# Moving the last tile's query projection ahead of the products with wo, and stacking the few-column products of each wp block

## The chip, the core and the metric

The kernel runs on one core of a Trainium2 chip. A core has a TensorE (matrix products, from SBUF into PSUM), a VectorE, a ScalarE and a GpSimd (elementwise work), and a SyncE whose queue issues most DMAs. In the profile these are PE (with its weight loads as PEld), DVE, ACT, POOL and SP. Each engine takes its instructions strictly in the order of the program and meets the others through semaphores. The metric is the device time of the whole kernel in microseconds; less is better.

## The reference

Two branches over the same 2048 tokens of width 576 are mixed by a gate. Branch A is a linear attention with 32 heads of 18 columns; branch B is a layer norm and an MLP with 4608 hidden columns.

```python
def _A_ref(x, wqkv, wo):
    q, k, v = ...                       # (x @ wqkv), 32 heads of 18 columns
    phi = lambda t: jnp.where(t > 0, t + 1, jnp.exp(t)) + 1e-6
    pq, pk = phi(q), phi(k)
    kv = jnp.einsum("bhsd,bhse->bhde", pk, v)
    z = jnp.einsum("bhsd->bhd", pk)
    num = jnp.einsum("bhqd,bhde->bhqe", pq, kv)
    den = jnp.einsum("bhqd,bhd->bhq", pq, z)[..., None] + 1e-6
    return (num / den).transpose(...).reshape(B, S, D) @ wo
...
g = _sigmoid((x * gate_w).sum(-1, keepdims=True))
return g * _A_ref(...) + (1 - g) * _B_ref(...)   # _B_ref: layernorm, w1, gelu, w2
```

## The kernel before

**Stages.** The 2048 tokens are 16 tiles of 128 rows. The first stage (to about 184 us) goes over the tiles: it projects keys and queries, applies phi, and sums two things over all tokens: the keys (for z) and the products of x with the keys. From these sums, `kv = wv^T (x^T phi(k))` needs no values of single tokens. Then comes the short middle stage, which the change concerns (about 184 to 206 us): it makes the block-diagonal kv of each head, multiplies it with wo into one matrix wp of 576 x 576, and so folds the value product and the output projection into one. The attention loop (lines 900 to 912, 16 turns) then multiplies each tile's normalized queries with wp. After it the MLP runs as a Strassen-like scheme with seven products, in an order that a planner writes out; the change does not touch that, and the planner's costs are constants.

**Splitting.** Most large products are kept near float32 accuracy: each factor is the sum of a rounded high part and a low part, and three products (high by high, high by low, low by high, `TERMS`) are summed in PSUM. A high part is a ScalarE copy, a low part a VectorE subtraction.

**Groups and blocks.** The 576 columns of kv are cut into groups of `GW = 126` = 7 heads of 18, so that no head straddles a group: four groups of 126, and a fifth that is laid over the last 126 columns. wp is cut into five blocks of 128 rows (the last has 64, kept twice for its high and low parts). Block t takes its rows from group t and, since 128 > 126, a few from group t+1: 2, 4, 6 and 8 rows for t = 0 to 3. `PIECES` (line 573) lists these nine pairs. `mask_kv` (653) multiplies kv, read from PSUM, with a block-diagonal mask into `kvs`; `kv_low` (663) makes the low parts; `project_values(t)` (764) does, for each half of 288 output columns, three products for each of the block's pieces, so 12 matmuls a block and 6 for the last, each with a weight load. ScalarE and VectorE then take block t out of PSUM as the high and low parts of wp.

**The order in the middle stage** (lines 666 to 810). TensorE: the queries of tile `late[1]`, kv (733 to 737: 25 products in float32, each two records), `project_values(0..4)`, the transposes of tile 0, the queries of tile `late[2]` (lines 804, 805; the last of three tiles whose queries were left over), the transposes of tile 1, then the loop. `normalize(i)` (693) makes the denominator of tile i (reduce, add, reciprocal: part 0) and multiplies it into the queries (part 1, a scalar_tensor_tensor on VectorE); `tail_q(i)` (705) copies the last 64 columns twice on ScalarE; `transpose_q(i)` (776) transposes the queries on TensorE and splits them into `qt` (high on ScalarE, low and tail on VectorE); `queries_out(i)` (343) is phi: for each half two passes on ScalarE and one on VectorE. `weigh(i)` (687) on GpSimd multiplies queries with z for the denominator; `qz` has three buffers, so weigh(4) waits until the reduce of normalize(1) has read its buffer, and weigh(5) until that of normalize(2) has.

**PSUM.** There are eight banks. project_values takes pairs of banks in turn, (6, 7) and (4, 5), and a pair is free again when VectorE has taken block t out; transposes use (0, 1) and (2, 3); attend uses (6, 7) and (4, 5).

**SBUF reuse and the queues.** High and low parts of wo lie where the key weights were; high parts of kv lie in the first of the four places for x; the low parts in a place of a finished store. On the SP queue come, in order: wo (at job 40), the stores of y, `load_w1(0)` (762), then `load_y` (811) over the same place, which waits for the products with wo. GpSimd has `sum_keys` of the last tiles, then `weigh(0)`.

Of the kernel before, what the change touches and what calls it, by code (L numbers as in the profile page):

```python
# [31 lines left out]
ORDER = [sup * TPS + a * TPB + j for sup in range(NSUP) for j in range(TPB) for a in range(2)]  # L32
PLACE = [ORDER.index(i) for i in range(NT)]
# [5 lines left out]
LATE = 3  # L39
X_RING = 4  # L40
# [54 lines left out]
def raw(ap):  # L95
    return ap.bitcast(F32)
# [35 lines left out]
def tile_gated_mix(ctx: ExitStack, tc: tile.TileContext, x, xm, xe, wm, we, wvm, wve, wo, um, ue, w2, b1, b2, gw, out):  # L132
    nc = tc.nc
    pe, act, dve, pool = (InOrder(tc, e) for e in (nc.tensor, nc.scalar, nc.vector, nc.gpsimd))
    sp = InOrder(tc, nc.sync)
# [5 lines left out]
    ps = ctx.enter_context(tc.tile_pool(name="ps", bufs=1, space=PSUM)).tile([P, 8, 512], F32, name="ps")  # L141
    t_pairs, ff_banks, ff_pairs = cycle((0, 2)), cycle(range(4)), cycle((6, 4))

    def two_of(ring):
        n = next(ring)
        return ps[:, n:n + 2]
# [36 lines left out]
    mask = spare[:GW, 26 * P:26 * P + GW]  # L183
# [18 lines left out]
    QUERY, KEY = range(2)  # L202
    TERMS = ((0, 0), (0, 1), (1, 0))
    W, at_ = {}, 0
    for part in (KEY, QUERY):
        for half in range(2):
            n = HALF + 2 * (part == KEY and half)
# [3 lines left out]
    y_place = ym[:, at_ + X_RING * 9 * P:][:, :2 * 5 * P]  # L211
    x_places = [ym[:, at_ + n * 9 * P:at_ + (n + 1) * 9 * P].rearrange("p (a n) -> p a n", n=P) for n in range(X_RING)]
# [3 lines left out]
    wv = a1.enter_context(tc.tile_pool(name="wvp", bufs=1)).tile([P, 5, D], F32, name="wv")  # L216
# [73 lines left out]
    def project(i, part, half, order=BY_ROWS, n=None, between={}):  # L290
        w = W[part, half]
        p = banks[i, part, half] = ps[:, next(halves_in) if n is None else n]
        for m, (a, b) in enumerate(order):
            pe.matmul(p[:, :w.shape[2]], xs[i][:, a, :], w[:, b], start=(m == 0), stop=(m == len(order) - 1))
            if m in between:
                between[m]()
# [46 lines left out]
    def queries_out(i):  # L343
        for half in range(2):
            phi(acc[i], i, QUERY, half)
# [223 lines left out]
    wop_ = wop.enter_context(tc.tile_pool(name="wop", bufs=1, side="right"))  # L569
    wot = wop_.tile([GW, G, D], F32, name="wot")  # L570


    PIECES = [(t, j) for t in range(5) for j in (t, t + 1) if j < G]
    kvs = wop_.tile([GW, len(PIECES), P], F32, name="kvs")
    pool.memset(kvs, 0.0)
    ysc = ExitStack()
    ysp = ysc.enter_context(tc.tile_pool(name="ysp", bufs=1, side="right"))
    y_stages = [ysp.tile([P, 2, 5, P], F32R, name=f"ys{n}") for n in range(3)]
# [5 lines left out]
    def at(n, f, *args):  # L584
        jobs[n].append(lambda: f(*args))

    def load_wo():
        sp.dma_start(wot[:, 0:4], wo[0:4 * GW].rearrange("(t p) n -> p t n", p=GW))
        sp.dma_start(wot[:, 4], wo[D - GW:D])

    def load_wv():
        sp.dma_start(wv[:, 0:4], wvm.rearrange("p (t n) -> p t n", t=4))
        load_twice(wv[:, 4], wve)

    at(3 * 5, sp.dma_start, b1s, b1)
    at(9, load_wv)
    at(40, load_wo)
    for b, n in enumerate((9, 13, 22, 28)):
# [20 lines left out]
    for n in range(FIRST, NT):  # L619
        i, before = ORDER[n], ORDER[n - 1]  # L620
# [22 lines left out]

    late, end = ORDER[NT - LATE:], ORDER[-1]
    wo_parts = [ym[:GW, a * G * D:(a + 1) * G * D].rearrange("p (j n) -> p j n", j=G) for a in range(2)]
    kv_parts = [x_places[PLACE[late[0]] % X_RING - 1][:GW], y_place[:GW, :len(PIECES) * P].rearrange("p (t n) -> p t n", n=P)]

    def split_wo(j0, j1):
        hi, lo = (part[:, j0:j1] for part in wo_parts)
        act.activation(hi, wot[:, j0:j1], AF.Copy)  # L650
        dve.tensor_sub(lo, wot[:, j0:j1], raw(hi))

    def mask_kv(n0, n1):
        for n in range(n0, n1):
            t, j = PIECES[n]
            c0 = min(j * GW, D - GW)
            lo, hi = max(j * GW, t * P), min((j + 1) * GW, (t + 1) * P, D)
            own = slice(lo - c0, hi - c0)
            for at_ in (lo - t * P, lo - t * P + 64)[:1 + (t == 4)]:
                dve.tensor_tensor(out=kvs[:, n, at_:at_ + hi - lo], in0=kv[j][:, own], in1=mask[:, own], op=OP.mult)  # L660
        act.activation(kv_parts[0][:, n0:n1], kvs[:, n0:n1], AF.Copy)

    def kv_low(n0, n1):
        dve.tensor_sub(kv_parts[1][:, n0:n1], kvs[:, n0:n1], raw(kv_parts[0][:, n0:n1]))

    split_wo(0, 2)
    split_wo(2, 4)
    projected(late[0], QUERY)
    queries_out(late[0])
    split_wo(4, 5)  # L670
    moments_of(end)
    for part in range(2):
        add_products(end, part)
# [31 lines left out]
    def tail_q(i):
        tails[i] = small.tile([P, P], F32, name="tail")
        act.activation(halves(tails[i]), acc[i][:, None, 4 * P:D].to_broadcast([P, 2, 64]), AF.Copy)


    xk = spare[:, :5 * D].rearrange("p (t n) -> p t n", n=D)  # L710
# [19 lines left out]
    dve.tensor_scalar(den0, den0, EPS_PHI, EPS_PHI, op0=OP.mult, op1=OP.add)  # L730
    project(late[1], QUERY, 0, n=4)
    project(late[1], QUERY, 1, n=0)
    kv = [ps[:GW, 1 + j // 3, j % 3 * GW:(j % 3 + 1) * GW] for j in range(G)]
    for j in range(G):
        c0 = min(j * GW, D - GW)
        for t in range(5):
            pe.matmul(kv[j], wv[:, t, c0:c0 + GW], xk[:, t, c0:c0 + GW], start=t == 0, stop=t == 4)
    queries_out(late[1])
    for i in range(1, 3):
        weigh(i)  # L740
    normalize(0, (0,))
    mask_kv(0, 5)
    normalize(0, (1,))
    tail_q(0)
    kv_low(0, 5)
    mask_kv(5, 9)
    kv_low(5, 9)
    w_pairs = cycle((6, 4))

    def wr(k):  # L750
        at_ = fresh[:, :21 * P] if k > 1 else spare[:, :21 * P]
# [12 lines left out]
    def project_values(t):  # L764

        pw = two_of(w_pairs)
        own = [(n, j) for n, (to, j) in enumerate(PIECES) if to == t]
        for half in range(2):
            parts = [(kv_parts[a][:, n], wo_parts[b][:, j]) for a, b in TERMS for n, j in own]
            for m, (a, b) in enumerate(parts):  # L770
                pe.matmul(pw[:, half, :HALF], a, b[:, half_cols(half)], start=m == 0, stop=m == len(parts) - 1)
        p = pw[:, :, :HALF]
        act.activation(halves(wp[:, t]), p, AF.Copy)
        dve.tensor_tensor(out=halves(wp[:, 5 + t]), in0=p, in1=halves(raw(wp[:, t])), op=OP.subtract)

    def transpose_q(i):

        both = two_of(t_pairs)
        p, pe_ = both[:, 0].rearrange("p (g n) -> p g n", n=P), both[:, 1, :P]
        for t in range(4):  # L780
            pe.transpose(p[:, t, :], acc[i][:, t * P:(t + 1) * P], ident)
        pe.transpose(pe_, tails[i], ident)
        if i == LAST_SHARE:
            turn_moments(len(MOMENTS) - 1, both[:, 1, P:2 * P])
        q = qt[i] = qtp.tile([P, 9, P], F32R, name="qt")
        act.activation(q[:, 0:4], p, AF.Copy)
        if i == LAST_SHARE:
            store_moments(len(MOMENTS) - 1, both[:, 1, P:2 * P])
        act.activation(q[:, 4], pe_, AF.Copy)
        dve.tensor_sub(q[:, 5:9], p, raw(q[:, 0:4]))  # L790
        dve.scalar_tensor_tensor(q[:, 4], raw(q[:, 4]), low_half[:, 0:1], pe_, op0=OP.mult, op1=OP.add)

    project_values(0)
    normalize(1, (0,))
    project_values(1)
    project_values(2)
    project_values(3)
    normalize(1, (1,))
    project_values(4)
    tail_q(1)  # L800
    normalize(2, (0,))
    transpose_q(0)
    normalize(2, (1,))
    for half in range(2):
        project(late[2], QUERY, half, n=4 + half)
    transpose_q(1)
    tail_q(2)
    queries_out(late[2])
    a1.close()
    for m in [FACTORS[n][1] for n in UP_ORDER]:  # L810
        load_y(0, m)
# [874 lines left out]
```

## Time and profile before

| what | us |
|---|---|
| median of three runs (lowest, highest) | 1088.93 (1088.69, 1089.76) |
| the profiled execution's own time | 1087.51 |
| its span from first to last instruction | 1085.8 |
| PE busy (matmuls) | 1080.8 (100%) |
| PEld busy (weight loads) | 994.5 (92%) |
| DVE busy | 933.9 (86%) |
| ACT busy | 692.7 (64%) |
| POOL busy | 242.4 (22%) |

Times in the timeline count from the start of the span. A row of the timeline gives start, length, engine, operation, tiles, shape, count, and in brackets the idle time of the engine before it and who ended it. A row of the groups gives count, busy time, mean length of one in ns, and the idle time before. Nearly all lines are L125, a helper that records every operation, so rows are told apart by their tiles: `ps<-accs,wv` is kv, `ps<-y 126x288` the products with wo, `ps<-y 128x288` a query projection, `ps<-wp,qt` attend, `den<-qz` the reduce of normalize, `accs<-accs,den` its last step, `kvs<-ps,accs` the mask.

### The profile page before, as it was taken

To read this page: it belongs to the slowest core of one execution; us is meant where nothing else is said; L and a number is where in the kernel's file an instruction comes from. 1 tells how busy PE (TensorE), PEld (TensorE's weight loads), DVE (VectorE), ACT (ScalarE), POOL (GpSimd) and SP (SyncE) were. 2 spreads that over 40 slices of the span, in tenths; PEclk is the share of its full clock that TensorE was granted. 3 is DMA by queue.
4 is the path that set the end of the run, shared out by engine and by line. 5 is a ranking of instruction groups with operands and counts; after the bars stand their busy time and mean duration, and the time that the engine had idled before them with its cause. 6 is when DMAs were issued, how large, how long until landed. Compare 5 with 4: busy or idle time off the path is not lost.

```text
span 1085.8 us, 18609 instructions
## 1 busy us (share of the span) xinstructions
PE 1080.8 (100%) x6700; PEld 994.5 (92%) x6700; DVE 933.9 (86%) x1547; ACT 692.7 (64%) x1234; POOL 242.4 (22%) x226
## 2 busy tenths in 40 slices
PE   9999999999999999999999999999999999999998
PEld 9999999999898999998899989998999989999898
DVE  5568787895799999899999998988878888888898
ACT  7677766444668777778887785555545455455642
POOL 2111112431123231322323321121231132112100
PEclk9999999999999999999999999999999999999999
DMA  6356662735744746664656559764544445344432
GB/s 188 126 97 183 177 215 105 311 149 193 246 157 174 248 163 225 202 211 165 205 192 220 180 190 385 244 226 119 158 121 125 119 135 150 119 120 119 142 94 88
DMA packets 116062, 189.65 MB, mean 175 GB/s; under 512 B 8956, under 2 KB 79244, under 8 KB 111874
## 3 DMA queue, kind: packets, MB, share of 16 engines
q1 hardware_dynamic: 115074, 187.72, 53.6%
q8 instruction: 53, 0.87, 0.3%
q10 hardware_dynamic: 704, 0.74, 0.2%
q14 instruction: 39, 0.32, 0.1%
q0 software_dynamic: 192, 0.01, 0.1%
HBM read 121.63 MB, written 66.80 MB: 174 GB/s over the span
## 4 chain that ended last, share of the span: by engine, by line
PE 99%; DVE 0%; ACT 0%; issue 0%
PE ps L125 99%; DVE wp L125 0%; ACT wp L125 0%; DVE ystage L125 0%; DVE ones L125 0%
## 5 line engine op out<-in xcount | busy, mean ns | idle before, releaser
L125 PEld LDWEIGHTS ps<-region,h 128*128 128x128 f32 x3060 | 434.3, 188 | 25.2 <-issue 0.8
L125 PE MATMUL ps<-region,h 128*128 128x288 f32 x3060 | 450.7, 295 | 0.0
L125 DVE TENSOR_TENSOR accs<-ps,accs 128x576 f32<-128x576 f32 x337 | 249.5, 752 | 44.3 <-PE ps L125 37.5
L125 PE MATMUL ps<-y,wa 128*128 128x512 f32 x1008 | 254.9, 392 | 0.0
L125 PEld LDWEIGHTS ps<-y,wa 128*128 128x128 f32 x1008 | 181.9, 188 | 31.8
L125 PE MATMUL ps<-y,wb 128*128 128x512 f32 x756 | 198.6, 393 | 0.0
L125 DVE TENSOR_TENSOR h<-u,h 128x512 fp32r<-128x512 f32 x243 | 170.4, 721 | 7.3 <-ACT u L125 6.8
L125 POOL TENSOR_TENSOR fresh<-fresh 128x288 f32<-128x288 f32 (+1 forms) x99 | 87.5, 886 | 325.4 <-DVE h L125 99.0
L125 PEld LDWEIGHTS ps<-y,wb 128*128 128x128 f32 x756 | 133.8, 188 | 20.7
L125 POOL TENSOR_TENSOR u<-u 128x512 f32<-128x512 f32 x67 | 92.9, 1387 | 245.5 <-ACT u L125 57.9
L125 PE MATMUL ps<-y 128*128 128x288 f32 (+2 forms) x950 | 133.2, 297 | 0.2 <-DVE wp L125 0.2
L125 PEld LDWEIGHTS ps<-y 128*128 128x128 f32 (+1 forms) x950 | 129.7, 188 | 1.8 <-DVE wp L125 0.9
L125 ACT ACTIVATE ps<-ps 128x512 f32<-128x512 f32 (+1 forms) x129 | 79.9, 622 | 72.2 <-PE ps L125 45.0
L125 ACT ACTIVATE region<-fresh 128x576 fp32r<-128x576 f32 (+1 forms) x134 | 82.3, 624 | 62.5 <-PE ps L125 61.5
L125 ACT ACTIVATE u<-ps 128x512 f32<-128x512 f32 x73 | 43.4, 595 | 77.9 <-PE ps L125 76.7
L125 ACT ACTIVATE h<-u 128x512 fp32r<-128x512 f32 x132 | 77.7, 622 | 20.0 <-POOL u L125 10.6
L125 DVE TENSOR_TENSOR region<-fresh,region 128x576 fp32r<-128x576 f32 (+1 forms) x134 | 87.7, 684 | 0.0
L125 DVE TENSOR_TENSOR u<-ps,u 128x512 f32<-128x512 f32 x74 | 50.3, 681 | 15.1 <-PE ps L125 12.8
L125 PE MATMUL ps<-wp,qt 128*128 128x288 f32 x448 | 63.0, 297 | 0.0
L125 ACT ACTIVATE h<-u,b1s 128x512 fp32r<-128x512 f32 x73 | 52.5, 720 | 13.3 <-DVE u L125 12.9
L125 PEld LDWEIGHTS ps<-wp,qt 128*128 128x128 f32 x448 | 59.8, 188 | 0.0
L125 PE MATMUL ps<-ks,xs 128*128 128x448 f32 (+4 forms) x256 | 53.4, 354 | 0.0
(140 smaller groups left out, 1042.2 us busy)
## 6 DMA issues: line engine op xcount, KB each, us to landing
w1d<-wa SPq DMA_DIRECT2D x17, 1280.0 KB
wa<-w1d SPq DMA_DIRECT2D x68, 320.0 KB
fresh<-in_w SPq DMA_DIRECT2D x70, 288.0 KB
y<-yd SPq DMA_DIRECT2D x14, 1280.0 KB
w1d<-wb SPq DMA_DIRECT2D x17, 960.0 KB
wb<-w1d SPq DMA_DIRECT2D x51, 320.0 KB
fresh<-in_um SPq DMA_DIRECT2D x64, 128.0 KB
yd<-ys SPq DMA_DIRECT2D x12, 640.0 KB
```

Source lines behind the costliest of these rows:

```text
L125: self.last = self.tc.keep_in_program_order(op(*args, **kwargs))
```

## The change

1. The fifth group no longer overlaps the fourth: `SIZES` is 126, 126, 126, 126, 72. The kv product of the fifth group has 72 columns, and wo and kv are cut to match.
2. The three products with group t+1 become one. Its first 18 rows (one head) suffice. `rest_kv` and `rest_wo` hold three bands of 18 rows, at partitions 0, 32 and 64: kv high with wo high, kv low with wo high, kv high with wo low. One product over 96 rows sums all three. A block has 8 matmuls rather than 12; the last stays at 6.
3. `rest_wo` is first filled by GpSimd copies, twice (jobs 44 and 47, and again after `split_wo(4, 5)`), so that the rows between bands are defined; six DMAs on the SP queue (`gather_rest`) then bring the bands from the split wo. The rows of kv between bands are zeros.
4. `mask_kv` goes block by block and has one VectorE copy more for blocks 1 to 4; the few columns get ScalarE copies (two each call of `kv_high`) and a VectorE subtraction of their own.
5. The queries of `late[2]` go right behind kv on TensorE, to banks 0 and 3. Their phi, normalize(1) in one piece and tail_q(1) come ahead of the products with wo; normalize(2) in one piece comes behind them and ahead of the transposes of tiles 0 and 1, which now follow one another.
6. The products with wo take a third pair of banks in turn, (1, 2).

```diff
-    PIECES = [(t, j) for t in range(5) for j in (t, t + 1) if j < G]
-    kvs = wop_.tile([GW, len(PIECES), P], F32, name="kvs")
+    SIZES = [min(GW, D - j * GW) for j in range(G)]
+    kvs = wop_.tile([GW, G, P], F32, name="kvs")
     pool.memset(kvs, 0.0)
+    rest = wop_.tile([DH, G - 1, 8], F32, name="rest")
+    pool.memset(rest, 0.0)
+    rest_wo = wop_.tile([96, G - 2, D], F32R, name="rest_wo")
...
+    kv_place = x_places[PLACE[ORDER[NT - LATE]] % X_RING - 1]
+    rest_kv = kv_place[:96, G:]
+    rest_wo_last = y_place[:96, G * P:G * P + D]
+    at(44, pool.tensor_copy, rest_wo, wot[:96, :G - 2])
+    at(47, pool.tensor_copy, rest_wo_last, wot[:96, G - 2])
+    at(47, pool.tensor_copy, rest_kv, kvs[:96, :G - 1])
...
+    def gather_rest():
+        for at_, part in ((0, 0), (32, 0), (64, 1)):
+            sp.dma_start(raw(rest_wo[at_:at_ + DH]), raw(wo_parts[part][:DH, 1:G - 1]))
+            sp.dma_start(raw(rest_wo_last[at_:at_ + DH]), raw(wo_parts[part][:DH, G - 1]))
+
+    def mask_kv(t):
+        lo, hi = t * P - t * GW, min((t + 1) * P - t * GW, SIZES[t])
+        for at_ in (0, 64)[:1 + (t == 4)]:
+            dve.tensor_tensor(out=kvs[:SIZES[t], t, at_:at_ + hi - lo], in0=kv[t][:, lo:hi], in1=mask[:SIZES[t], lo:hi], op=OP.mult)
+        if t:
+            n = 2 * t
+            dve.tensor_copy(rest[:, t - 1, 8 - n:], kv[t][:DH, :n])
+
+    def kv_high(t0, t1):
+        n = SIZES[t1 - 1]
+        act.activation(kv_parts[0][:n, t0:t1], kvs[:n, t0:t1], AF.Copy)
+        r0, r1 = max(t0 - 1, 0), t1 - 1
+        for at_ in (0, 64):
+            act.activation(rest_kv[at_:at_ + DH, r0:r1, P - 8:], rest[:, r0:r1], AF.Copy)
...
     split_wo(4, 5)
+    pool.tensor_copy(rest_wo, wot[:96, :G - 2])
+    pool.tensor_copy(rest_wo_last, wot[:96, G - 2])
+    gather_rest()
+    pool.tensor_copy(rest_kv, kvs[:96, :G - 1])
...
+    for half in range(2):
+        project(late[2], QUERY, half, n=3 * half)
     normalize(0, (0,))
-    mask_kv(0, 5)
+    for t in range(3):
+        mask_kv(t)
     normalize(0, (1,))
+    mask_kv(3)
+    kv_high(0, 4)
     tail_q(0)
-    kv_low(0, 5)
-    mask_kv(5, 9)
-    kv_low(5, 9)
-    w_pairs = cycle((6, 4))
+    mask_kv(4)
+    kv_low(0, 4)
+    kv_high(4, 5)
+    kv_low(4, 5)
+    w_pairs = cycle((6, 4, 1))
...
-            parts = [(kv_parts[a][:, n], wo_parts[b][:, j]) for a, b in TERMS for n, j in own]
+            parts = [(kv_parts[a][:n, t], wo_parts[b][:n, t]) for a, b in TERMS]
+            if t < 4:
+                parts.append((rest_kv[:, t], rest_wo[:, t] if t < 3 else rest_wo_last))
...
-    project_values(0)
-    normalize(1, (0,))
-    project_values(1)
-    project_values(2)
-    project_values(3)
-    normalize(1, (1,))
-    project_values(4)
+    normalize(1)
     tail_q(1)
-    normalize(2, (0,))
-    transpose_q(0)
-    normalize(2, (1,))
-    for half in range(2):
-        project(late[2], QUERY, half, n=4 + half)
-    transpose_q(1)
+    queries_out(late[2])
+    for t in range(5):
+        project_values(t)
+    normalize(2)
+    for i in range(2):
+        transpose_q(i)
     tail_q(2)
-    queries_out(late[2])
```

More of the change, by code (lines that the diff above doesn't have):

```diff
@@ L588, in load_wo @@
         sp.dma_start(wot[:, 0:4], wo[0:4 * GW].rearrange("(t p) n -> p t n", p=GW))
-        sp.dma_start(wot[:, 4], wo[D - GW:D])
+        sp.dma_start(wot[:SIZES[4], 4], wo[4 * GW:D])
     def load_wv():
@@ L645, in tile_gated_mix @@
     wo_parts = [ym[:GW, a * G * D:(a + 1) * G * D].rearrange("p (j n) -> p j n", j=G) for a in range(2)]
-    kv_parts = [x_places[PLACE[late[0]] % X_RING - 1][:GW], y_place[:GW, :len(PIECES) * P].rearrange("p (t n) -> p t n", n=P)]
+    kv_parts = [kv_place[:GW, :G], y_place[:GW, :G * P].rearrange("p (t n) -> p t n", n=P)]
     def split_wo(j0, j1):
-        hi, lo = (part[:, j0:j1] for part in wo_parts)
-        act.activation(hi, wot[:, j0:j1], AF.Copy)
-        dve.tensor_sub(lo, wot[:, j0:j1], raw(hi))
@@ L653, in mask_kv @@
[L653 to L661, printed above, removed]
@@ L663, in kv_low @@
-    def kv_low(n0, n1):
-        dve.tensor_sub(kv_parts[1][:, n0:n1], kvs[:, n0:n1], raw(kv_parts[0][:, n0:n1]))
+        n = SIZES[j1 - 1]
+        hi, lo = (part[:n, j0:j1] for part in wo_parts)
+        act.activation(hi, wot[:n, j0:j1], AF.Copy)
+        dve.tensor_sub(lo, wot[:n, j0:j1], raw(hi))
+    def gather_rest():
+        for at_, part in ((0, 0), (32, 0), (64, 1)):
+            sp.dma_start(raw(rest_wo[at_:at_ + DH]), raw(wo_parts[part][:DH, 1:G - 1]))
+            sp.dma_start(raw(rest_wo_last[at_:at_ + DH]), raw(wo_parts[part][:DH, G - 1]))
@@ L666, in tile_gated_mix, with kv_low @@
+    def kv_low(t0, t1):
+        n = SIZES[t1 - 1]
+        dve.tensor_sub(kv_parts[1][:n, t0:t1], kvs[:n, t0:t1], raw(kv_parts[0][:n, t0:t1]))
+        r0, r1 = max(t0 - 1, 0), t1 - 1
+        dve.tensor_sub(rest_kv[32:32 + DH, r0:r1, P - 8:], rest[:, r0:r1], raw(rest_kv[:DH, r0:r1, P - 8:]))
     split_wo(0, 2)
@@ L732, in tile_gated_mix @@
     project(late[1], QUERY, 1, n=0)
-    kv = [ps[:GW, 1 + j // 3, j % 3 * GW:(j % 3 + 1) * GW] for j in range(G)]
-    for j in range(G):
-        c0 = min(j * GW, D - GW)
+    kv = [ps[:n, 1 + j // 3, j % 3 * GW:j % 3 * GW + n] for j, n in enumerate(SIZES)]
+    for j, n in enumerate(SIZES):
+        own = slice(j * GW, j * GW + n)
         for t in range(5):
-            pe.matmul(kv[j], wv[:, t, c0:c0 + GW], xk[:, t, c0:c0 + GW], start=t == 0, stop=t == 4)
+            pe.matmul(kv[j], wv[:, t, own], xk[:, t, own], start=t == 0, stop=t == 4)
     queries_out(late[1])
@@ L766, in project_values @@
         pw = two_of(w_pairs)
-        own = [(n, j) for n, (to, j) in enumerate(PIECES) if to == t]
+        n = SIZES[t]
         for half in range(2):
-            parts = [(kv_parts[a][:, n], wo_parts[b][:, j]) for a, b in TERMS for n, j in own]
+            parts = [(kv_parts[a][:n, t], wo_parts[b][:n, t]) for a, b in TERMS]
+            if t < 4:
+                parts.append((rest_kv[:, t], rest_wo[:, t] if t < 3 else rest_wo_last))
             for m, (a, b) in enumerate(parts):
```

## The prediction

> **What bounds the kernel now.** I read the page first, then the chain of work that ended last, then the timeline of the middle stage. Busy times on the page (us, share of the span, instructions), then two pieces of the chain (start, length, what):
>
> ```profile
> span 1085.8 us, 18609 instructions
> ...
> PE 1080.8 (100%) x6700; PEld 994.5 (92%) x6700; DVE 933.9 (86%) x1547; ACT 692.7 (64%) x1234; POOL 242.4 (22%) x226
> ```
>
> ```profile
> 1.13 193.47 PE ps L125 x1301
> ...
> 198.03 884.16 PE ps L125 x5376
> ```
>
> TensorE sets the end; only near 194 to 198 us does the chain leave it. So a microsecond won or lost in the middle stage is one at the end, as long as TensorE stays the bound behind it. Matmul busy time hides waits, since matmuls overlap; the weight loads show them. Their timeline in that stage:
>
> ```profile
> 183.75 4.39 PEld L125 LDWEIGHTS ps<-accs,wv 128*126 128x126 f32 x39
> ...
> 189.27 3.30 PEld L125 LDWEIGHTS ps<-y 126*128 126x128 f32 x24
> ...
> 192.74 1.62 PEld L125 LDWEIGHTS ps<-y 126*128 126x128 f32 x12 [0.17 <-DVE wp L125]
> ...
> 194.62 2.43 PEld L125 LDWEIGHTS ps<-y 126*128 126x128 f32 x18 [0.27 <-DVE wp L125]
> ...
> 198.02 3.74 PEld L125 LDWEIGHTS ps<-y 128*128 128x128 f32 x28 [0.42 <-DVE wp L125]
> ...
> 201.71 0.49 PEld L125 LDWEIGHTS ps<-accs 128*128 128x128 f32 x4
> ...
> 202.28 3.74 PEld L125 LDWEIGHTS ps<-wp,qt 128*128 128x128 f32 x28
> ...
> 205.96 0.49 PEld L125 LDWEIGHTS ps<-accs 128*128 128x128 f32 x4
> ```
>
> In order: kv from 183.75, the products with wo from 189.27, the queries of the last tile at 198.02, the transposes of tile 1 at 201.71, attend(0) at 202.28, the next turn's transposes at 205.96. That last time is the one I carry through: before, attend(0) is over at 205.96. TensorE waits 0.17 + 0.27 + 0.42 = 0.86 in all, each time for VectorE to take a block of wp out of a pair of banks. One product of 288 columns takes (205.96 - 202.28) / 28 = 0.131; with the small irregularities I use 0.133. A kv record takes (4.39 - 0.19) / 38 = 0.11.
>
> **The change on TensorE alone.** The sixteen products fewer (4 blocks, 12 to 8) give 16 x 0.133 = 2.13. The fifth group of kv has 10 records of 72 columns where there were 126. No row has that width: between 0.11 (nothing won) and 0.063 (in proportion, 0.11 x 72/126) each; I take 0.07, nearer the proportional end since 0.11 and 0.131 already rise with the columns: 0.4, bounds 0 and 0.47. With the three waits gone, 2.13 + 0.4 + 0.86 = 3.4. A TensorE that never waited would be 3.4 us earlier. Everything below asks whether the other engines let it.
>
> **VectorE and ScalarE.** The rows that price their work, first those of the timeline, then the groups of 180 to 205 us (count, busy us, mean ns, idle before):
>
> ```profile
> 187.38 0.81 DVE L125 TENSOR_TENSOR kvs<-ps,accs 126x126 f32<-126x126 f32 x5 [0.65 <-PE ps L125]
> ...
> 188.10 0.75 DVE L125 SCALAR_TENSOR_TENSOR accs<-accs,den 128x576 f32<-128x576 f32 x1
> ...
> 192.60 0.74 DVE L125 TENSOR_REDUCE den<-qz 128x32 f32<-128x576 f32 x1
> ...
> 193.38 0.19 DVE L125 TENSOR_TENSOR den<-den,den 128x32 f32<-128x32 f32 x1
> 193.42 1.44 POOL L125 TENSOR_TENSOR qz<-accs,pks 128x576 f32<-128x576 f32 x1 [5.81 <-DVE den L125]
> 193.60 0.35 DVE L125 RECIPROCAL den<-den 128x32 f32<-128x32 f32 x1
> ...
> 201.04 0.34 DVE L125 SCALAR_TENSOR_TENSOR qt<-qt,low_half,ps 128x128 fp32r<-128x128 f32 x1
> ...
> 214.57 1.43 POOL L125 TENSOR_TENSOR qz<-acc,pks 128x576 f32<-128x576 f32 x1 [1.76 <-DVE den L125]
> ...
> 215.14 1.48 DVE L125 SCALAR_TENSOR_TENSOR accs<-accs,den 128x576 f32<-128x576 f32 x1
> ...
> 215.50 0.20 ACT L125 ACTIVATE g<-g 128x8 f32<-128x8 f32 x1
> ```
>
> ```profile
> L125 DVE TENSOR_TENSOR wp<-ps,wp 128x576 fp32r<-128x576 f32 x5 | 3.7, 743 | 2.0 <-ACT wp L125 1.9
> L125 ACT ACTIVATE wp<-ps 128x576 fp32r<-128x576 f32 x5 | 3.3, 652 | 3.6 <-PE ps L125 3.5
> ...
> L125 ACT ACTIVATE e<-e 128x288 f32<-128x288 f32 x4 | 1.8, 445 | 0.1
> L125 ACT ACTIVATE e<-ps 128x288 f32<-128x288 f32 x4 | 1.6, 408 | 1.4 <-PE ps L125 1.4
> L125 DVE SCALAR_TENSOR_TENSOR acc<-ps,e 128x288 f32<-128x288 f32 x3 | 1.4, 453 | 1.5 <-ACT e L125 1.5
> L125 DVE TENSOR_TENSOR qt<-ps,qt 128x512 fp32r<-128x512 f32 x2 | 1.3, 660 | 1.0 <-ACT qt L125 1.0
> ...
> L125 ACT ACTIVATE tail<-accs 128x128 f32<-128x128 f32 x3 | 0.9, 311 | 0.7 <-DVE accs L125 0.7
> ...
> L125 DVE TENSOR_TENSOR y<-kvs,y 126x512 fp32r<-126x512 f32 x1 | 0.7, 692 | 0.7 <-ACT y L125 0.7
> ...
> L125 ACT ACTIVATE y<-kvs 126x512 fp32r<-126x512 f32 x1 | 0.6, 632 | 1.3 <-DVE kvs L125 1.3
> ...
> L125 DVE TENSOR_TENSOR kvs<-ps,accs 126x2 f32<-126x2 f32 x1 | 0.1, 150 | 0.0
> ```
>
> One pair of rows matters more than its size. The last step of normalize takes 0.75 at 188.10, and 1.48 at 215.14, where a GpSimd product started at 214.57 and ended at 216.00: the step ends 0.62 after the product. The reduce of normalize frees a `qz` buffer and so starts weigh (193.42, right behind the reduce that ended at 193.34); in the loop the last step, about 0.65 behind the reduce, runs into it. Before, normalize(1) and normalize(2) were cut in two, and so normalize(1) got out of its way. In one piece both will meet it: 1.49 each rather than 0.75. [...]
>
> Now step by step, in order of each engine, with some 0.03 for each hop between engines.
>
> 1. Masks 0 to 2 and normalize(0) stay where they are (187.38, 188.10). Mask 3 waits for the bank of groups 3 and 4, whose last record now issues near 188.8 and ends near 189.25. Mask 3 (0.27), kv high on ScalarE (0.63), kv low (0.69), then block 4 in the same way on 128 columns, with six ScalarE copies (0.20 by the 128x8 row, partly overlapped) and eight VectorE ones (0.15, issuing every 0.07) of the few columns: VectorE gets to normalize(1) at 191.15. The small ones lie on this path with about 0.4; at nothing or double, the end is 0.4 earlier or later.
> 2. normalize(1): reduce to 191.9, weigh(4) on GpSimd from then to 193.4, last step from 192.55 to 194.05.
> 3. ScalarE's next instruction is tail_q(1), which waits for that step. Behind it are queued the four passes of phi of the last tile (TensorE has its halves ready by 191.2 and 193.0), and behind them the wp high parts. 194.07 + 0.3 + 2 x (0.41 + 0.45), overlapped: phi ends at 195.95.
> 4. TensorE: queries of the last tile 188.87 to 192.6 (28 x 0.133); blocks 0, 1, 2 to 195.8. Block 3 takes the first pair of banks again. Its high part is taken at 195.86 to 196.51, its low part at 196.54 to 197.3. **TensorE waits 1.55 until 197.35.** Blocks 3 and 4 then end at 199.2 (14 x 0.133), two tiles' transposes (0.57 each, 202.28 - 201.71) at 200.35.
> 5. High part of block 4: 199.55 to 200.2; low part to 201.0. Then normalize(2), ahead of tile 0's qt in VectorE's order: reduce to 201.65, weigh(5) to 203.15, last step 202.3 to 203.8. Then qt's low part (0.66) and tail (0.34): **done at 204.65**. Before this was done at 201.04 + 0.34 = 201.38.
> 6. attend(0) starts at 200.75, makes the 8 of the first half's 14 products that need only the high parts of qt, waits from 201.8 to 204.7, and makes the other 20: 204.7 + 2.66 = **207.35, 1.4 later than 205.96**.
>
> So the 3.4 gained are eaten by waits of 1.55 and 2.9, plus the hops. Put another way: the query projection covered VectorE's work on wp and qt before; now it covers kv and normalize(1), and nothing covers the rest.
>
> **Other moved work that I cost at nothing.** VectorE in the loop has room behind a TensorE turn of 4.25 (205.96 - 202.28 and 0.57 of transposes), by the row of that stretch (PE, PEld, DVE busy of 40.00); it ends phi earlier than before and reaches normalize(3) at 205.4, as before. So the 1.4 is carried on, neither grown nor won back.
>
> ```profile
> 200.00:240.00 40.00, 40.00 (x313) 39.98 (x312) 36.06 (x72) 19.07 (x45) 18.07 (x13) 1.00 0.68 274
> ```
>
> GpSimd's copies (2816 columns, twice) and the six DMAs lie here:
>
> ```profile
> 174.64 0.45 DVE L125 SCALAR_TENSOR_TENSOR acc<-ps,e 128x288 f32<-128x288 f32 x1
> ...
> 178.55 0.87 PEld L125 LDWEIGHTS ps<-pks,ones 128*128 128x128 f32 x4
> ...
> 181.90 5.72 POOL L125 TENSOR_TENSOR qz<-accs,pks 128x576 f32<-128x576 f32 x4 [11.07 <-ACT pks L125]
> ...
> 191.46 0.55 SPq L125 DMA_DIRECT2D accs<-in_ue  x1
> ...
> 195.36 1.02 POOL L125 TENSOR_TENSOR accs<-accs 128x384 f32<-128x384 f32 x1 [0.50 <-DMA accs<-in_ue]
> ```
>
> ```profile
> L125 POOL COPY pks<-k 128x576 f32<-128x576 f32 x1 | 0.7, 667 | 10.1 <-DVE k L125 10.1
> ```
>
> By 667 ns for 576 columns they take 3.3 a time; the first 2.0 fall before 169, the other 4.6 into the 11.07 idle ahead of weigh(0). At the price of a two-input product (1.43 for 576) it would be 9.7, still inside. What they may block on VectorE there (split of wo, phi of the first late tile) has 3.4 us until the product with ones takes the same banks (174.64 + 0.45 to 178.55); the copies beside it last 3.3, so without that cover it would be up to 3 on the path. The DMAs come ahead of load_w1(0), which goes out only as kv ends; a load issued by 192.0 had landed by 195.36, so 3.4 at most, and theirs from about 177.5 have until 192.6. load_y waits for the products with wo about 2 longer and is not needed until the sixteen turns are over.
>
> **The rivals.**
> - *The collisions with GpSimd do not come* (a w1 sum holds weigh back, or it starts after the last step): 0.74 off for each; one gone gives +0.65, both -0.1. For it: GpSimd waited for a DMA at 195.36. Against: weigh(4) has nothing ahead of it by 191.9. Time 1088.8 to 1089.6.
> - *VectorE and ScalarE keep up*: their work is hidden and TensorE runs without waits. 1088.93 - 3.4 = 1085.5; with the wait at block 3 but not at attend, 1087.1. For it: the third pair of banks and the cut in matmuls are real. Against: steps 3 and 5, which are a fixed order.
> - *Slower: attend(0) waits as a whole.* If its first product waits for all of qt, the eight early ones come behind 204.7 too: 204.7 + 28 x 0.133 = 208.4, +2.5, so 1091.4. It decides whenever qt is written after 200.75. For it: before, qt was done (201.38) ahead of attend(0) (202.28), so no row shows a partial start. Against: the loads of the kernel's start are cut in pieces as though parts were waited for.
> - That the sixteen matmuls do not go is excluded by the code; that they are worth less than 0.133 each is not seen in any row.
>
> **How the numbers follow.** The profiled execution took 1087.51, 1.7 beyond its span; the median of the runs is 1088.93, 1.42 above it. The difference of +1.4 goes onto the median: **1090.3**. Chances: the forecast 0.53 (its own range 1089.7 to 1091.4), collisions absent 0.22, engines keep up 0.10, attend waits as a whole 0.15. A measurement of this kernel tells about 0.2%, 2.2 us, from no change. Faster by more (below 1086.75): 0.10. Slower by more (above 1091.1): 0.15 and a tail of 0.08 of the forecast (small copies and hops at double), 0.23. Within: 0.67. Range 1088.0 to 1092.2: it takes in the collisions' absence, the whole wait, and 0.8 of small costs on top.
>
> **What would show it.** Right: weight loads of block 3 waiting about 1.5 for VectorE's wp; the last steps of normalize(1) and (2) at about 1.49 beside GpSimd; a wait of about 3 inside attend(0), ended by VectorE's qt; the next turn's transposes near 207.4. Wrong: these near 203 (engines keep up), at 206 (no collisions), or one wait ahead of attend(0)'s first product. PE waits before 183 us would show that GpSimd's copies do cost something.

## The result, and the profile after

| | before | changed |
|---|---|---|
| median of 11 runs (lowest, highest) | 1088.73 (1088.31, 1089.76) | 1091.17 (1090.41, 1093.08) |
| ratio, 95% interval | | 1.0024, 1.0016 to 1.0032 |
| the profiled execution's own time | 1087.51 | 1090.82 |

The changed kernel is 0.24% slower, 2.6 us by the ratio and 2.4 by the medians: inside the range, 0.9 above the predicted 1090.3, and beyond the 0.2% bound on the slow side, though the interval still takes that bound in. Medians and ratios in this document leave out two slow executions, one of e10 (1776.13) and one of the kernel before (2163.02). The page of the changed kernel:

```profile
span 1088.7 us, 18604 instructions
...
PE 1079.8 (99%) x6684; PEld 992.7 (91%) x6684; DVE 939.5 (86%) x1549; ACT 692.4 (64%) x1238; POOL 250.8 (23%) x233
```

TensorE does the sixteen matmuls less (6700 to 6684) and is busy 1.0 us less, yet the span is 2.9 longer (0.9 of this is the late start of kv, see below). The weight loads of the changed kernel's middle stage (start, length, instruction, count, idle before and who ended it):

```profile
184.66 5.19 PEld L125 LDWEIGHTS ps<-accs,wv 128*126 128x126 f32 x50
...
198.61 1.90 PEld L125 LDWEIGHTS ps<-y 126*128 126x128 f32 x14 [1.90 <-DVE wp L125]
...
201.97 1.09 PEld L125 LDWEIGHTS ps<-wp,qt 128*128 128x128 f32 x8 [0.37 <-ACT qt L125]
...
205.89 2.70 PEld L125 LDWEIGHTS ps<-wp,qt 128*128 128x128 f32 x20 [2.83 <-DVE qt L125]
...
208.54 0.49 PEld L125 LDWEIGHTS ps<-accs 128*128 128x128 f32 x4
```

Where the kernel before waited three times for 0.86 in all, there are now waits of 1.90 at block 3 of wp, 0.37 ahead of attend(0), and 2.83 inside it, behind eight of its products. The work of VectorE, ScalarE and GpSimd that ends them, on the same time line:

```profile
191.01 0.69 DVE L125 TENSOR_TENSOR y<-kvs,y 126x512 fp32r<-126x512 f32 x1 [0.30 <-ACT y L125]
...
192.45 0.75 DVE L125 TENSOR_REDUCE den<-qz 128x32 f32<-128x576 f32 x1
...
193.28 1.43 POOL L125 TENSOR_TENSOR qz<-accs,pks 128x576 f32<-128x576 f32 x1 [4.77 <-DVE den L125]
...
193.85 1.48 DVE L125 SCALAR_TENSOR_TENSOR accs<-accs,den 128x576 f32<-128x576 f32 x1
...
195.37 0.31 ACT L125 ACTIVATE tail<-accs 128x128 f32<-128x128 f32 x1 [3.17 <-DVE accs L125]
...
197.79 2.09 DVE L125 TENSOR_TENSOR wp<-ps,wp 128x576 fp32r<-128x576 f32 x3
...
202.14 0.74 DVE L125 TENSOR_REDUCE den<-qz 128x32 f32<-128x576 f32 x1
...
202.96 1.41 POOL L125 TENSOR_TENSOR qz<-accs,pks 128x576 f32<-128x576 f32 x1 [5.56 <-DVE den L125]
...
203.53 1.46 DVE L125 SCALAR_TENSOR_TENSOR accs<-accs,den 128x576 f32<-128x576 f32 x1
...
204.91 0.68 DVE L125 TENSOR_TENSOR qt<-ps,qt 128x512 fp32r<-128x512 f32 x1
...
205.51 0.33 DVE L125 SCALAR_TENSOR_TENSOR qt<-qt,low_half,ps 128x128 fp32r<-128x128 f32 x1
```

ScalarE stands idle for 3.17 in front of tail_q(1) with phi queued behind it; the last steps of both normalizations (193.85 and 203.53) take twice their 0.75 beside GpSimd's products (193.28 and 202.96); tile 0's split comes behind normalize(2).

**How the runs are compared below.** The length of the middle stage, from the first weight load of kv to the transposes of the second turn, is 205.96 - 183.75 = 22.21 before and 208.54 - 184.66 = 23.88 after: +1.67. This leaves out that the changed kernel's profile is 0.9 late already when kv begins. Each stage is read from one profile; those of e1 and e3 are of executions with a mean granted clock of 0.998, the others of executions at 0.999 or 1.0.

The stage can't show what lies outside the span. The device time exceeds the span of its execution by 1.7 to 1.8 in every execution, where the span is known, of the kernels without the stacked product (before, e1, e11), and by 1.9 to 3.4, in the median 2.0 to 2.3, in those with it. So about 0.5 of device time goes with the stacked product, whatever the order. No run takes this apart.

### The profile page after: what moved, and what is told of

It is laid out like the page before. It is cut to its first block, busy times and chain, and to the rows that moved or that the text cites. A ratio compares the mean times of both kernels' runs of the same rounds, so it can differ in the third digit from the quotient of the medians.

```text
span 1088.7 us, 18604 instructions
## 1 busy us (share of the span) xinstructions
PE 1079.8 (99%) x6684; PEld 992.7 (91%) x6684; DVE 939.5 (86%) x1549; ACT 692.4 (64%) x1238; POOL 250.8 (23%) x233
## 4 chain that ended last, share of the span: by engine, by line
PE 98%; DVE 1%; ACT 0%; issue 0%; ACTq 0%
PE ps L125 98%; DVE accs L125 0%; DVE den L125 0%; DVE wp L125 0%; DVE y L125 0%; ACT wp L125 0%; ACT e L125 0%; DVE qt L125 0%; ACT y L125 0%; DVE ystage L125 0%; ACT tail L125 0%; DVE kvs L125 0%; DVE ones L125 0%; ACTq L125 0%
## 5 line engine op out<-in xcount | busy, mean ns | idle before, releaser
L125 PE MATMUL ps<-y 128*128 128x288 f32 (+2 forms) x928 | 130.6, 296 | 1.7 <-DVE wp L125 1.7
L125 PEld LDWEIGHTS ps<-y 128*128 128x128 f32 (+1 forms) x928 | 127.0, 188 | 2.9 <-DVE wp L125 1.9
```

The costliest lines, as they stand in the source:

```text
L125: self.last = self.tc.keep_in_program_order(op(*args, **kwargs))
```

## The experiments

Two theories went in. **A**: the order on VectorE and ScalarE makes the waits, and the stacked product is worth what it saves once nothing waits. **B**: the stacked product, with its copies, casts and DMAs, is what costs. A third, **C**, on the clock, came with e6. Each kernel was timed in turns with the kernel before on the same chip. "Beyond the span" is the median of device time less span. The diffs are condensed: several statements stand on a line. All results:

| kernel | ratio to before (95%) | median us | middle stage | against 22.21 | beyond the span |
|---|---|---|---|---|---|
| changed | 1.0024 (1.0016 to 1.0032) | 1091.17 | 23.88 | +1.67 | 2.2 |
| e1 order alone | 1.0035 (1.0023 to 1.0048) | 1092.90 | 26.11 | +3.90 | 1.7 |
| e2 stacked product alone | 1.0008 (0.9999 to 1.0017) | 1089.62 | 22.59 | +0.38 | 2.2 |
| e3 normalize(2) last | 1.0013 (1.0004 to 1.0022) | 1090.02 | 23.44 | +1.23 | 2.2 |
| e4 reduces earlier | 1.0005 (0.9996 to 1.0015) | 1089.55 | 22.12 | -0.09 | 2.2 |
| e5 phi first | 1.0025 (1.0014 to 1.0037) | 1092.00 | 22.81 | +0.60 | 2.3 |
| e6 waits filled | 1.0019 (1.0010 to 1.0028) | 1090.68 | 23.87 | +1.66 | 2.2 |
| e7 no waits | 0.9983 (0.9975 to 0.9992) | 1086.83 | 20.09 | -2.12 | 2.3 |
| e9 no waits, second order | 0.9978 (0.9969 to 0.9988) | 1086.38 | 19.45 | -2.76 | 2.2 |
| e10 one batch of copies | 0.9979 (0.9970 to 0.9988) | 1086.74 | 19.44 | -2.77 | 2.0 |
| e11 twelve products | 0.9995 (0.9986 to 1.0004) | 1088.37 | 21.65 | -0.56 | 1.7 |

### e1: the order alone

```diff
 # the kernel before, with the order, banks and third pair of the change
+    for half in range(2):
+        project(late[2], QUERY, half, n=3 * half)
     normalize(0, (0,))
...
-    project_values(0) ... queries_out(late[2])
+    normalize(1); tail_q(1); queries_out(late[2])
+    for t in range(5): project_values(t)
+    normalize(2); transpose_q(0); transpose_q(1); tail_q(2)
```

> The kernel before with the changed order alone (last tile's queries behind kv, normalize(1), tail_q(1) and phi ahead of the products with wo, normalize(2) behind them, third pair of banks), the twelve products a block as before, no stacked product, no GpSimd copies, no gather DMAs. Theory A (order of VectorE and ScalarE makes the loss): TensorE waits about 0.3 at block 3 and about 3 inside attend(0), and the sixteen products are not saved: 2.6 us slower than before (2.0 to 3.2), so slower than the changed kernel. Theory B (the stacked product with its copies, six DMAs and small casts makes the loss): within 0.7 of before.

Measured: 1.0035, the slowest of all. Theory B is out as the main cause: without any stacked product the loss is larger. Inside attend(0) TensorE waits 2.83, as expected; at block 3 its loads show no wait where 0.3 was expected. But +3.90 is beyond A's own range (2.0 to 3.2). Weight loads and the windows of 4 us (PE, PEld, DVE, ACT, POOL busy, the granted clock, then the DMA engines) of e1:

```profile
206.71 4.22 PEld L125 LDWEIGHTS ps<-wp,qt 128*128 128x128 f32 x20 [2.83 <-DVE qt L125]
```

```profile
203.00:207.00 4.00, 1.40 (x10) 1.17 (x10) 3.90 (x8) 0.87 (x3) 2.89 (x2) 1.00 1.01 416
207.00:211.00 4.00, 4.00 (x21) 4.00 (x21) 3.19 (x6) 0.00 (x0) 2.75 (x2) 0.57 1.01 428
211.00:215.00 4.00, 4.00 (x34) 4.00 (x33) 2.38 (x6) 1.60 (x4) 0.96 (x2) 1.00 1.00 422
```

The same 20 products that took 2.70 in the changed kernel take 4.22: **behind the wait of 2.83 the granted clock falls to 0.57 over 4 us**. Without these 1.5 the stage is +2.4, as A had it. Four of e1's five executions have a mean granted clock of 0.997 or 0.998; the one at 1.0 took 1091.30, which is 2.4 above the kernel before in the same turns (1088.88).

### e2: the stacked product alone

```diff
 # the changed kernel, with the order of before (last tile's queries between
 # the transposes, normalize(1) and (2) cut in two)
-    w_pairs = cycle((6, 4, 1))
+    w_pairs = cycle((6, 4))
```

> The changed kernel with the order of before put back (products with wo right behind kv, last tile's queries between the transposes of tiles 0 and 1, normalize(1) and (2) cut in two, two pairs of banks), the stacked product and all its copies kept. Theory A: without the queries ahead of it, block 0 of wp waits for the masked kv and its low and stacked parts (about 2 us on TensorE), so that most of the 2.5 saved goes there: 0.7 us slower than before (-0.5 to +1.3). Theory B: 1.5 to 2.5 slower. A third reading, that the stacked product pays in the old order: 1.5 to 2.5 faster.

Measured: 1.0008, A's 0.7 by the medians; the interval, -0.1 to 1.9, rules the third reading out and only just reaches into B's 1.5 to 2.5. The agreement with A's 0.7 is in part luck: the stage is +0.38, and some 0.5 lies beyond the span. The weight loads show why the sixteen matmuls bring nothing there:

```profile
191.69 0.30 PEld L125 LDWEIGHTS ps<-y 126*128 126x128 f32 x2 [1.18 <-ACT y L125]
192.41 0.19 PEld L125 LDWEIGHTS ps<-y 126*128 126x128 f32 x1 [0.43 <-DVE y L125]
...
195.22 0.43 PEld L125 LDWEIGHTS ps<-y 126*128 126x128 f32 x3 [0.70 <-DVE wp L125]
...
197.10 1.90 PEld L125 LDWEIGHTS ps<-y 126*128 126x128 f32 x14 [0.79 <-DVE wp L125]
```

Right behind kv, block 0 waits for the high and then the low parts; blocks 2 and 3 for the pairs of banks: 3.1 together, where the kernel before waits 0.44 there. The two halves of the change lean on each other.

### e3: normalize(2) behind the transposes

```diff
-    normalize(2)
     for i in range(2):
         transpose_q(i)
+    normalize(2)
     tail_q(2)
```

> The changed kernel with normalize(2) moved behind the transposes of tiles 0 and 1 and their split, nothing else. Theory A: the wait inside attend(0) goes from 2.8 to next to nothing, attend(0) ends about 2.7 earlier, but the transposes of tile 2 then wait about 1.2 for normalize(2): 1.5 us faster than the changed kernel, 0.1 slower than before (-0.4 to +0.8). Theory B (the loss lies in the stacked product or ahead of the middle stage): no more than 0.3 away from the changed kernel, so about 2.2 slower than before.

Measured: 1.0013, by its interval 0.4 to 2.4 us above before, with the expected +0.1 just outside. The wait inside attend(0) went, and the one for normalize(2) came (0.94 for 1.2), both as expected. What was not:

```profile
199.24 3.10 PEld L125 LDWEIGHTS ps<-y 126*128 126x128 f32 x14 [1.90 <-DVE wp L125]
202.29 0.82 PEld L125 LDWEIGHTS ps<-accs 128*128 128x128 f32 x4
...
204.03 3.75 PEld L125 LDWEIGHTS ps<-wp,qt 128*128 128x128 f32 x28 [0.27 <-ACT qt L125]
208.73 0.42 PEld L125 LDWEIGHTS ps<-accs 128*128 128x128 f32 x4 [0.94 <-DVE accs L125]
```

```profile
200.00:203.00 3.00, 3.00 (x15) 2.98 (x14) 1.28 (x2) 0.92 (x2) 0.00 (x0) 0.50 0.09 14
```

Behind the 1.90 at block 3 the clock is at 0.50, and 14 products take 3.10 rather than 1.90. Less that 1.2 and the 0.33 on the transposes, the stage would be near 22; this is an estimate, as later waits might have grown. The spans bear it out: six of the eleven executions have a mean clock of 0.998, with a median span of 1088.1, and the five at 1.0 have 1087.3, 0.1 above the kernel before in the same turns (1087.2). So the expected +0.1 is there in the span; the clock and the 0.5 beyond the span make the rest.

### e4: the reduces earlier

```diff
     mask_kv(4)
+    normalize(1, (0,))
     kv_low(0, 4)
...
-    normalize(1)
+    normalize(1, (1,))
...
+    normalize(2, (0,))            # between blocks 2 and 3
     ...
-    normalize(2)
+    normalize(2, (1,))
```

> The changed kernel with the reduces of normalize(1) and (2) taken earlier (between the mask and the low part of kv; behind block 2 of wp), so that GpSimd's weigh no longer runs beside their last steps. The work of VectorE is the same. Theory A: the last step of normalize(1) takes 0.75 in place of 1.48, block 3 waits about 0.7 to 1.2 less, the wait inside attend(0) is 1.5 shorter: 2.1 us faster than the changed kernel, 0.6 faster than before (-1.1 to +0.2). If the collision with GpSimd cost nothing: within 0.5 of the changed kernel.

Measured: 1.0005. Over the changed kernel this is 2.1 us won by the ratios ((1.0024 - 1.0005) x 1089), with 2.1 expected, but that agreement is partly luck: the stage is 1.76 shorter, and none of e4's executions has the lower clock that five of the changed kernel's have. The median lies 0.5 to 0.8 above the kernel before, where 0.6 below was expected; the stage is -0.09, not -0.6, and the 0.5 beyond the span comes on top. VectorE in e4:

```profile
192.27 1.53 DVE L125 TENSOR_TENSOR y<-kvs,y 126x512 fp32r<-126x512 f32 x1
...
194.55 0.76 DVE L125 SCALAR_TENSOR_TENSOR accs<-accs,den 128x576 f32<-128x576 f32 x1
```

The last step is back at 0.76, but **the collision went to the subtraction now beside GpSimd's product: 1.53 where it took 0.69**. The reduce that frees the product's buffer ended at 191.74; with the 0.08 and the 1.43 of the changed kernel (193.28) the product ran from 191.82 to 193.25, an estimate, and the subtraction ended at 193.80. Both instructions read two operands from SBUF. The low parts of wp, which read one operand from PSUM, did not lengthen: in e7 one took 0.74 (197.81) beside a GpSimd product (197.24, 1.92 long). That the place of the operands makes the difference is the author's reading; no run changes it alone. So block 3 still waited (1.50). The gain came at attend(0), 1.47 in place of 2.83.

### e5: phi ahead of the last step of normalize(1)

```diff
-    normalize(1)
-    tail_q(1)
+    normalize(1, (0,))
     queries_out(late[2])
+    normalize(1, (1,))
+    tail_q(1)
```

> The changed kernel with phi of the last tile put between the reduce and the last step of normalize(1), and tail_q(1) behind that step: ScalarE no longer queues phi behind a copy that waits for normalize(1); normalize(2) stays ahead of tile 0's split. Theory A: block 3 of wp waits 0.2 to 0.7 in place of 1.8 and the last step of normalize(1) takes about 0.75, while the wait inside attend(0) stays at 2.7 to 3.3: 0.8 to 1.5 us faster than the changed kernel, about 1.2 slower than before. If the queue on ScalarE were not the cause of the wait at block 3: no change against the changed kernel.

Measured: 1.0025, no gain in the median. The weight loads agree with A all the same:

```profile
198.13 1.90 PEld L125 LDWEIGHTS ps<-y 126*128 126x128 f32 x14 [0.84 <-DVE wp L125]
...
205.42 2.69 PEld L125 LDWEIGHTS ps<-wp,qt 128*128 128x128 f32 x20 [2.84 <-DVE qt L125]
```

Block 3 waits 0.84 instead of 1.90 (0.2 to 0.7 expected), attend(0) as long as before, and the stage is 1.07 shorter than the changed kernel's. Two things went at once: phi no longer queues behind tail_q(1), and the last step of normalize(1), now behind GpSimd's product, is back near 0.75. This is an estimate: 1.18 lie between the end of phi's last pass on ScalarE (195.26) and tail_q(1) (196.44), and phi's own step on VectorE, 0.46 in the changed kernel, takes its part of them. So e5 does not tell the queue from the collision. The runs fall in two: three at a mean granted clock of 1.0 took 1089.54, 1089.75 and 1090.84, about what was expected; four at 0.997 to 0.998 took 1092.00 to 1092.77.

### e6: the waits filled with products nobody reads

```diff
+    def fill(bank_, n):
+        for _ in range(n):
+            pe.matmul(ps[:, bank_, :P], ones, ones, start=True, stop=True)
     for t in range(5):
+        if t == 3:
+            fill(0, 6)
         project_values(t)
...
             for n, (a, b) in enumerate(BY_ROWS):
+                if i == 0 and half == 0 and n == 8:
+                    fill(4, 10)
```

> The changed kernel with 16 products of ones with ones put into TensorE's two waits (6 ahead of block 3 of wp, 10 ahead of the product of attend(0) that waits), about 1.3 and 2.2 us of work that nothing reads; all else as in the changed kernel. Theory C (TensorE falls to half its clock for some us behind a wait of 2 to 3 us in part of the executions, as the profiles of the order alone and of normalize(2) behind the transposes show with products of 0.240 us): with the waits filled the clock stays, so the slower executions go: highest within 1.0 of the lowest, median 0.4 to 0.8 below the changed kernel, about 1.8 slower than before. If the clock has no part in it: median as the changed kernel's (+2.4) or slower, spread 2.5 us as there.

This tests theory C: behind a long wait (2.83 in e1, 1.90 in e3) TensorE falls to half its clock (0.50 in e3) in part of the executions. Measured: the stage is unchanged (23.87), the waits left in the two places are 0.29 and 0.20 around the first filling and 0.57 behind the second, and

| | runs | mean granted clock 0.997 to 0.998 | at 0.999 or 1.0 |
|---|---|---|---|
| changed | 11 | 5, median 1092.18 | 6, median 1090.74 |
| e6 | 11 | none | 11, median 1090.68 |

With the waits filled no run falls to the lower clock; the spread is 1.28 in place of 2.67 (a little over the 1.0 expected). Adding work took nothing and on the median gave 0.5. So the lower clock goes with the waits: theory C. Not all of the spread is the clock's: one execution of the changed kernel at 1.0 took 1091.97, with 3.3 beyond its span. By the spans the two groups are apart: 1088.2 to 1088.7 at full clock, 1089.0 to 1090.9 below it, with medians 1.0 apart.

All runs together, by the longest wait in this stage, with the executions at a mean clock of 0.997 or 0.998:

| longest wait | kernels | at the lower clock |
|---|---|---|
| 1.90 to 2.84 | changed, e1, e3, e5, e12 | 19 of 35 |
| 0.37 to 1.50 | e2, e4, e6, e7, e9, e10, e11 | 0 of 75 |

### e7, e9: the same work without the waits

```diff
+    normalize(1, (0,))
+    normalize(2, (0,))
+    queries_out(late[2])
+    project_values(0)
+    normalize(1, (1,))            # e9: behind block 1
+    project_values(1)
+    tail_q(1)                     # e9: behind block 2
+    for t in range(2, 5): project_values(t)
+    for i in range(2): transpose_q(i)
+    normalize(2, (1,))
+    tail_q(2)
```

> The changed kernel with another order of the middle stage: the reduces of normalize(1) and (2) behind the low parts of kv, then phi of the last tile, block 0 of wp, the last step of normalize(1), block 1, tail_q(1), blocks 2 to 4, the transposes of tiles 0 and 1 with their split, and only then the last step of normalize(2). Same work on every engine. Theory A: no wait of TensorE over 0.5, attend(0) starts 3 earlier than in before: 2.0 to 3.0 us faster than before, ratio 0.9972 to 0.9982. Theory B (the stacked product costs by itself): not faster than before.

> As the order without waits, with the last step of normalize(1) one block later (behind block 1 of wp, so that it no longer meets the w1 sum on GpSimd, beside which it took 1.52 there) and tail_q(1) behind block 2. Theory A: the wait of 0.93 at block 4 goes; 0.5 to 0.9 faster than that order, so 2.3 to 2.9 faster than before (ratio 0.9973 to 0.9979).

Measured: e7 0.9983, just short of its range (0.9972 to 0.9982); e9 0.9978, as expected. In e7 (timeline of all engines) one collision was left, and with it a wait of 0.87 where none over 0.5 was expected:

```profile
196.26 1.01 POOL L125 TENSOR_TENSOR accs<-accs 128x384 f32<-128x384 f32 x1 [1.57 <-PE ps L125]
196.38 1.51 DVE L125 SCALAR_TENSOR_TENSOR accs<-accs,den 128x576 f32<-128x576 f32 x1
...
198.61 0.56 PEld L125 LDWEIGHTS ps<-y 72*128 72x128 f32 x4 [0.87 <-DVE wp L125]
```

e9 takes the step past it. Its weight loads:

```profile
184.64 5.19 PEld L125 LDWEIGHTS ps<-accs,wv 128*126 128x126 f32 x50
...
200.18 1.09 PEld L125 LDWEIGHTS ps<-wp,qt 128*128 128x128 f32 x8 [0.53 <-ACT qt L125]
201.46 2.68 PEld L125 LDWEIGHTS ps<-wp,qt 128*128 128x128 f32 x20 [0.19 <-DVE qt L125]
...
204.09 0.49 PEld L125 LDWEIGHTS ps<-accs 128*128 128x128 f32 x4
```

0.72 of waiting is left. e9 beats both kernels: 2.4 us below before and, by medians of different turns, 4.8 below the changed kernel, with the changed kernel's instructions in another order. All of its runs had a mean granted clock of 1.0.

### e10, e11: what the copies cost, what the stacked product is worth

```diff
 # e10: e9 without
-    at(44, pool.tensor_copy, rest_wo, wot[:96, :G - 2])
-    at(47, pool.tensor_copy, rest_wo_last, wot[96, G - 2])
-    at(47, pool.tensor_copy, rest_kv, kvs[:96, :G - 1])
 # e11: the kernel before, in the order of e9
```

> The kernel of e9 without the first batch of GpSimd's copies (jobs 44 and 47); the second batch, which writes the same places, stays. If the copies are hidden, as the prediction had it: within 0.4 of e9. If they slow VectorE on a path that counts: over 0.5 faster than e9.

> The order of e9 with the twelve products a block and the overlapping fifth group of before: no stacked product, no copies, no gather DMAs. Theory A: with no waits in the way the sixteen products and the narrower kv are worth what the prediction's first sum says: 1.8 to 2.6 slower than e9, so 0.0 to 0.8 faster than before. If the stacked product is worth nothing even there: as e9.

Measured: e10 is as e9 (0.9979 and 0.9978, stages 19.44 and 19.45; the medians are 0.36 apart, within the 0.4 expected): the first batch of copies is hidden. e11 is 0.9995, 2.0 slower than e9 by the medians and 2.20 by the stage, as expected: this is the worth of the smaller matmul work, net of what it costs beyond the span in the first figure. The order alone, done right, gives about 0.5, and its interval (-0.4 to 1.5) includes no gain at all.

### e8, e12: both kernels once more

> The kernel before once more, for a second profile. If the 0.9 us by which every profile of a changed kernel is late at 24 us already comes from the start of the execution and not from the change, this profile begins kv near 184.5 to 185.3, not 183.75. If it comes from the change: 183.75 again.

```profile
185.17 5.60 PEld L125 LDWEIGHTS ps<-accs,wv 128*126 128x126 f32 x50
...
207.38 0.49 PEld L125 LDWEIGHTS ps<-accs 128*128 128x128 f32 x4
```

The kernel before began kv at 185.17 this time (own time 1089.12), later than any changed kernel but e2, e3 and e5. The 0.9 is the first profile's early start; the stage is again 22.21.

> The changed kernel once more, for a second profile. Theory C: it either shows full clock all through and a time near 1090.5, or products of 0.240 us for up to 3.4 us behind the wait at block 3 or inside attend(0) and a time 1.0 to 1.6 longer, near 1092. If the longer times have another cause, a time near 1092 comes with full clock in the middle stage.

Waits of 1.90 and 2.84, a stage of 23.86, a mean granted clock of 1.0, and 1091.07: a little over the 1090.5 expected. The fall of the clock itself was seen in the profiles of e1 and e3; both profiles of the changed kernel are at full clock, and there only the mean over a run shows it.

## Why the prediction was right, and where it was off

**Direction and mechanism held.** TensorE's first sum (3.4 to be won) is borne out by e9 and e11: 2.76 of it shows once most of the waiting is gone, and e9 still waits 0.72. Its two terms: 16 x 0.133 = 2.13 and 0.4 for kv make 2.5, e9 against e11 gives 2.20, and e11 waits 0.35 less than e9. The bound on the 72 columns was on the right side: fifty records take 5.19 where they took 5.60, so 0.41 (0.40 predicted).

**Step 1** was mis-sized. From the first load of kv, VectorE was to reach normalize(1) at 191.15 - 183.75 = 7.4; it did at 192.45 - 184.66 = 7.79. Between the end of the first low part (191.70) and the reduce stand 0.75. Of these the two small subtractions make 0.17 + 0.16 and the hops about 0.1, so the small ones were sized about right at 0.4. What was too small is the rest: the step's own terms, 189.25 + 0.27 + 0.63 + 0.69 + 0.4, make 191.24 already, over the 191.15 that it states, and leave nothing for block 4's low part, which took 0.29 on this path:

```profile
191.73 0.17 DVE L125 TENSOR_TENSOR y<-rest,y 18x24 fp32r<-18x24 f32 x1
...
191.94 0.29 DVE L125 TENSOR_TENSOR y<-kvs,y 72x128 fp32r<-72x128 f32 x1
...
192.26 0.16 DVE L125 TENSOR_TENSOR y<-rest,y 18x8 fp32r<-18x8 f32 x1
```

**Step 2** held: 1.48 and 1.46 for 1.49, each behind weigh. **Step 3** held: 3.17 of idle time on ScalarE, and e5 shows that this queue and the collision together make over half of block 3's wait (1.90 to 0.84). How it divides between the two stays open: e4 took the collision off one instruction and put it on another. The rival *collisions do not come* fell at once.

**Step 4**: 1.55 predicted, 1.90 measured. **Step 5**: qt done 20.9 behind the start of kv predicted, 205.84 - 184.66 = 21.18 measured. **Step 6**: a partial start of attend(0) with 8 products, then a wait of 2.9, measured 2.83. So the rival *attend(0) waits as a whole* fell, and its 1091.4 came close to the result for another reason. End of the stage: 23.60 predicted (207.35 - 183.75), 23.88 measured. *VectorE and ScalarE keep up* is what e9 makes true, and it needs another order.

**Moved work at no cost**: right for TensorE, which waits 0.25 in all between 30 and 183 us, as before. GpSimd's copies in the changed kernel end 3.47 ahead of weigh(0), and e10 finds nothing for one batch of the two:

```profile
174.23 1.63 POOL L125 CAST rest_wo<-wot 96x1728 fp32r<-96x1728 f32 x1
...
177.54 1.73 POOL L125 CAST y<-kvs 96x512 fp32r<-96x512 f32 x1
182.74 4.19 POOL L125 TENSOR_TENSOR qz<-accs,pks 128x576 f32<-128x576 f32 x3 [3.47 <-ACT pks L125]
```

VectorE did pay: the low parts of the first four groups of wo took 4.52 beside the copies (at 174.28) where they took 2.62 before (at 172.10), but TensorE had no wait from it.

**What the sum lacked.** Of the 2.4 between the medians, 1.4 was predicted and 0.3 more is in steps 1 to 5. The forecast put two further things at nothing. The first is the clock: at a full one the median is 1090.74, over all 1091.17, so 0.4. The step "the 1.4 is carried on, neither grown nor won back" failed there: it treated a wait as lost time alone, while with waits of 1.90 and 2.83 the mean clock was also lower in 5 of 11 executions. The page of before gave no sign, with no wait over 0.42 in this stage; a chance for it would have put the forecast on the slow side of 0.2%, where I had 0.23. The second is the time beyond the span: the forecast carried the 1.7 of before over, and the changed kernel has 2.2, so 0.5. With both the sum is 2.6, 0.2 over the 2.4; its parts come from one profile and from medians, which need not add up. Theory B has this much right: some 0.5 goes with the stacked product, and its cause stays open.

## What to carry to other kernels

A block of TensorE work set between two stages covers the vector work of one side only: moving it uncovers the other, so count what each engine has to do, in its own order, until TensorE needs it. Fewer matmuls paid here (2 us) only after the order let them; first place reduces, casts and copies where nobody queues behind them, then cut. When GpSimd's work starts behind an instruction that you move, look for whatever two-operand SBUF instruction now runs beside it (0.75 became 1.48 here, and 0.69 became 1.53). Compare the time beyond the span as well as the stage: a change can cost there what no stage shows (0.5 here).

## What the runs showed of the hardware

**The clock fell behind waits of 1.90 and 2.83 us.** In e3 the granted clock is 0.80 over 199 to 200 us, 0.50 over 200 to 203 and 0.99 over 203 to 204. At 0.50 this makes 3.4 us, from 0.4 behind the end of the wait of 1.90 (199.24); both are estimates from these windows. 14 products take 3.10 instead of 1.90, by the same estimate about 0.24 each at the lower clock. In e1 the clock is 0.57 over 207 to 211, behind the wait of 2.83: again 3.4 us if it was at 0.50. In the changed kernel 5 of 11 executions have a lower mean clock, and their spans are 1.0 longer; with products of no use in the waits none has. Kernels whose longest wait in this stage was 1.50 or less had it in none of 75 executions. Why only some executions are hit, and what sets the length of the fall, no run shows.

**A VectorE instruction with two SBUF operands, issued behind a GpSimd product or sum, ended 0.5 to 0.6 behind it.** 0.75 became 1.48 and 1.46 in the changed kernel (at 193.85 and 203.53, each ending 0.62 behind the product) and 1.51 in e7 (at 196.38, 0.62 behind the sum). The subtraction in e4 went from 0.69 to 1.53, ending 0.55 behind the product by the estimate given there. GpSimd's times vary too: the same copy of 512 columns took 1.07 at 173.21 and 1.73 at 177.54, both in the changed kernel beside VectorE; what makes the difference, no run shows.
